# Attention and two expert layers on one core: weights and v scaled on the way to their fp16 halves

## The chip, the cores and the metric

The kernel runs on one core of a Trainium2 chip. The metric is the device time of one execution in microseconds (us), from the first to the last instruction with what the launch adds around them. Five engines work side by side: TensorE (PE, with its weight loads as PEld), VectorE (DVE), ScalarE (ACT), GpSimd (POOL) and SyncE (SP, which only issues transfers here).

## What is computed

The inputs come as float64 (the generator's weights) or float32 and the kernel keeps fp32-like precision by splitting each operand into two fp16 halves, a high and a low one, and multiplying three of the four pairs.

```python
def _attn_ref(q, k, v, proj):            # q, k, v: (2, 8, 768, 64)
    q_bits = (q @ proj > 0); k_bits = (k @ proj > 0)      # 6 bits: a bucket
    mask = q_bucket[:, :, :, None] == k_bucket[:, :, None, :]
    scores = np.where(mask, q @ k.T / sqrt(D), -1e9)
    return softmax(scores) @ v
def _moe_ref(x, w1, w2, w3, w_out):      # x: (1536, 512), d_ff 768
    h = np.maximum(np.maximum(x @ w1, x @ w2), x @ w3)
    return h @ w_out
def _moe2_ref(x, w_in, w_out):           # d_ff 2048
    h = x @ w_in
    return np.where(h > 0, h, np.exp(np.minimum(h, 0)) - 1) @ w_out
```

The output is `_moe2_ref(_moe_ref(_attn_ref(...)))`, 1536 x 512 in fp32.

## The kernel before

**Stages.** The tokens are cut into six chunks of 256. Attention runs over 24 units (a pair of heads of a chunk), four tiles each, 96 tiles of 128 queries in all. Per tile: four score matmuls on PE into the ring `s` (L646), the row maximum on DVE (L649), the scale and bias on DVE (L650, L652), the exponential on ACT into `P` (L654), the high half `hl` of `P` as a cast on ACT or DVE (L660, L662), the low half as a subtraction on POOL or DVE (L665), one transposing transfer `PT<-hl` (L667), and the products with v on PE (L676, L677). A chunk of four units is normalised, split, transposed into `xT`, and goes through the first expert layer (`plan_moe1`, matmuls at L714 with the operands `w` and `wot`). When all 96 tiles are done the attention's buffers are closed (`close_attn`) and the second layer (`plan_moe2`) runs over four groups of four 128-column slices of its weights, each group over the six chunks: matmuls L714 (`win`) and L848 (`wo2t`).

**Weights.** There are 56 weight tiles of 128x512 (18 of w1, w2, w3, 6 of `wot`, 16 of `win`, 16 of `wo2t`). They arrive as float64, 512 KB each. `plan_w` turns a tile into fp32: ACT writes a rebiased word `t1` (L558; the ring `dc1w` or `dc` in SBUF, two buffers), two half-word operations fill `t2` (L562 or L563, and L566 or L567, on ACT or DVE), and DVE joins `t1` and `t2` (L569). A norm follows (for the first 24 a Gram matrix on PE, L345; for the other 32 a square on ACT, L378) and from it a power-of-two scale. `plan_wsplit` then scales the tile in place (L580 on ACT or L581 on DVE), rounds it to the fp16 high half (L582, ACT or DVE), and subtracts to get the low half (L584, POOL or DVE). `plan_v` treats each of the eight 128x768 tiles of v alike (L524 to L527).

**Order.** Nothing here is ordered by hand. Every operation is declared with the engines it may run on, a cost on each, and a priority; a list scheduler (`Graph.schedule`) walks its own model of time, gives each engine the ready operation of the lowest priority number, and so fixes engine and order for the whole program before it runs. Each engine then runs its list in order. An operation marked `two=True` is one that the scheduler keeps from running on DVE while POOL works, unless `KAPPA` says that the delay is cheap. Rings limit what can run ahead: `mo`, three PSUM banks, is shared by the matmuls of both expert layers, the transposes of q and k, the Gram matrices and the norms.

**Line numbers.** In the changed file most lines after `plan_v` stand one line higher; L649 there is L648, L582 is L581 or L582, L584 is L583.

Of the kernel before, what the change touches and what calls it, by code (L numbers as in the profile page):

```python
# [233 lines left out]
KAPPA = 0.00184  # L234
# [4 lines left out]
def lsh_attention_moe_kernel(ctx: ExitStack, tc: tile.TileContext, q, k, v, proj,  # L239
# [80 lines left out]
    def sumsq(cols, prio, cap=False, also=(), x2=None, wt=None):  # L320
# [10 lines left out]
        op({"PE": 30 * (len(cols) + cap)}, mm, rd=[d for d, _ in cols], wr=[x2, c] + list(also), prio=prio + -6.12)  # L331
        return x2, c

    def gram(srcs, n, prio, cap=False, also=()):
# [13 lines left out]
        op({"PE": pe(len(srcs) * n // 128, 128)}, mm, rd=[b for b, _ in srcs], wr=[x2, m] + list(also), prio=prio + -10.78)  # L348
        op({"V": vred(128)}, lambda e: V.tensor_reduce(out=m.ap, in_=x2.ap[:, 0:128], op=ALU.max, axis=AX.X), rd=[x2], wr=[m], prio=prio + -0.87)
# [10 lines left out]
    def pow2(x2, s, inv, T, prio):  # L360
# [4 lines left out]
                                                       op0=ALU.logical_shift_right), rd=[x2], wr=[c], prio=prio + -9.83)  # L365
        op({"V": TINY}, lambda e: V.tensor_scalar(out=s[1]().bitcast(I32), in0=c.ap, scalar1=-u, scalar2=(189 + T) * u,
                                                  op0=ALU.mult, op1=ALU.add), rd=[c], wr=[s[0]], prio=prio + -1.03)
        op({"V": TINY}, lambda e: V.tensor_scalar(out=inv[1]().bitcast(I32), in0=c.ap, scalar1=u, scalar2=(65 - T) * u,
                                                  op0=ALU.mult, op1=ALU.add), rd=[c], wr=[inv[0]], prio=prio + 26.71)
# [4 lines left out]
    def square(src, sfn, n, acc, prio):  # L374
# [5 lines left out]
        op({"A": act(n, acc=1)}, f, rd=[src], wr=[acc[0]], prio=prio + -15.84)  # L380


    def plan_proj(prio):
        pr, acc, ps, pinv = tn(NB, "pr", 1), tn(1, "pacc", 1), tn(1, "ps", 1), tn(1, "pinv", 1)
        t0, t1 = tn(NB, "pt0", 1), tn(NB, "pt1", 1)
        op({"A": (640, 640, 30, -363.79)}, lambda e: A.dma_start(out=pr.ap[0:64], in_=proj), wr=[pr], prio=prio + -31.29)
        op({"A": (640, 640, 30, 99.65)}, lambda e: A.dma_start(out=pr.ap[64:128], in_=proj), wr=[pr], prio=prio + 49.41)
# [6 lines left out]
           rd=[pr, ps], wr=[t0], two=True, prio=prio + -24.51)  # L394
        op({"V": TINY}, lambda e: V.tensor_scalar(out=h[:, 0], in0=t0.ap, scalar1=-c, scalar2=None, op0=ALU.add),
           rd=[t0], wr=["prh0"], two=True, prio=prio + -184.42)
        op({"V": TINY}, lambda e: V.scalar_tensor_tensor(out=t1.ap, in0=pr.ap, scalar=ps.ap[:, 0:1], in1=h[:, 0],
                                                         op0=ALU.mult, op1=ALU.subtract), rd=[pr, ps, "prh0"], wr=[t1], two=True, prio=prio + -85.35)
        op({"V": TINY}, lambda e: V.tensor_copy(h[:, 1], t1.ap), rd=[t1], wr=["prh1"], two=True, prio=prio + -83.86)
        op({"V": TINY}, lambda e: V.tensor_tensor(out=h[:, 2], in0=t1.ap, in1=h[:, 1], op=ALU.subtract),  # L400
           rd=[t1, "prh1"], wr=["prh2"], two=True, prio=prio + -12.54)
# [398 lines left out]
    def plan_moe2(c, gi, fs, p0, dp):  # L800
# [54 lines left out]
        for j in range(QT):  # L855
# [8 lines left out]
            if gi == len(GROUPS) - 1:  # L864
                op({"D": (475, 450, 728)}, lambda e, j=j, ot=ot: SP.dma_start(out=dst[:, hf * QT + j, :], in_=ot.ap), rd=[ot], prio=pr + -42.11)
# [17 lines left out]
    for f in range(FM):  # L883
        plan_w13(f, CS + LM + 3 * f * DM1 - LW)
# [78 lines left out]
```

## Time and profile before

| | us |
|---|---|
| median of 3 runs (705.98 to 707.42) | 707.23 |
| the profiled execution's own time | 701.04 |
| its span, first to last instruction | 699.3 |
| PE busy | 623.1 (89%) |
| DVE busy | 580.2 (83%) |
| ACT busy | 495.0 (71%) |
| POOL busy | 287.3 (41%) |

The busy times of the table are sums over the whole span, while the stages are limited by different engines, so they are to be read per stretch: the page's slices (forty of 17.5 us each) and the windows (busy time of each engine in a stretch that one chooses) do that. The mean granted clock of TensorE is 0.941 of full speed. A row of instructions by line gives the count, the summed busy time and the mean duration of one; consecutive instructions of one engine overlap by about 0.1 us in these records, so sums of means are a little larger than the time that the engine was taken.

### The profile page before, as it was taken

Reading aid. Unit: us, or ns where it says so; the run is one execution under the profiler, and the core shown is the slowest. Engines: PE = TensorE matmul, PEld = TensorE weight load, DVE = VectorE, ACT = ScalarE, POOL = GpSimd, SP = SyncE. Lnnn points to the kernel's source line nnn. Section 1 sums busy time; section 2 is a strip of 40 time slices with the busy share of each in tenths; the row PEclk is TensorE's granted clock in tenths of the full one; section 3 lists DMA queues with packets and bytes.
Section 4 is the critical chain, followed back from the end, with each engine's and each line's share of the span. In section 5 each row is a group of like instructions: output and inputs, shape, how many; then the busy total and the mean of one; then the engine's idle time right before and its main releaser. Section 6 shows DMA issues by size and latency. Waiting matters only on the chain.

```text
span 699.3 us, 15296 instructions
## 1 busy us (share of the span) xinstructions
PE 623.1 (89%) x5658; PEld 473.4 (68%) x5658; DVE 580.2 (83%) x1594; ACT 495.0 (71%) x992; POOL 287.3 (41%) x231
## 2 busy tenths in 40 slices
PE   4586646878999969999999999999999999999997
PEld 3354434667788858888888887766666666666664
DVE  6798787978999969878999878778878978997774
ACT  4799999978998846775576369967945993763332
POOL 1366766556878743463454213512301440350000
PEclk9858677998899989999999999999999999999999
DMA  7899899995899868596798785311310210000112
GB/s 228 242 210 203 209 215 208 189 190 98 151 200 178 147 112 145 92 164 117 132 160 134 139 234 175 121 61 35 118 31 29 94 61 1 1 1 1 61 39 82
DMA packets 201210, 87.57 MB, mean 125 GB/s; under 512 B 167856, under 2 KB 195504, under 8 KB 201136
## 3 DMA queue, kind: packets, MB, share of 16 engines
q1 hardware_dynamic: 194768, 79.89, 54.0%
q10 hardware_dynamic: 6368, 6.70, 3.3%
q8 instruction: 44, 0.72, 0.4%
q14 instruction: 30, 0.25, 0.1%
HBM read 38.80 MB, written 3.15 MB: 60 GB/s over the span
## 4 chain that ended last, share of the span: by engine, by line
PE 65%; ACT 15%; DVE 8%; DMA 8%; issue 3%; POOL 0%; SPq 0%; ACTq 0%; DVEq 0%; POOLq 0%
PE mo L714 34%; PE out L848 17%; PE s L646 7%; PE o L676 3%; ACT P L654 3%; DMA PT<-hl 3%; DMA rawv<-in_v_dram 2%; ACT junk L378 2%; DMA raww<-in_moe_w_out_dram 2%; ACT hl L660 2%; PE o L677 2%; ACT dc2w L580 1%; DVE m L649 1%; PE mo L345 1%; PE mo L458 1%
## 5 line engine op out<-in xcount | busy, mean ns | idle before, releaser
L665 POOL TENSOR_TENSOR hl<-P,hl 128x768 f16<-128x768 f32 x80 | 135.5, 1699 | 100.8 <-ACT hl L660 66.6
L714 PE MATMUL mo<-xT,w 128*128 128x256 f16 x1296 | 154.0, 274 | 0.7 <-DVE hx L735 0.7
L714 PE MATMUL mo<-x1T,win 128*128 128x256 f16 x1152 | 140.6, 272 | 0.7 <-POOL win L584 0.7
L848 PE MATMUL out<-wo2t,gt 128*128 128x512 f16 x576 | 138.3, 379 | 0.0
L714 PEld LDWEIGHTS <-w 128*128 128x128 f16 x1296 | 123.8, 98 | 18.5 <-issue 2.0
L714 PEld LDWEIGHTS <-win 128*128 128x128 f16 x1152 | 111.0, 98 | 31.5 <-issue 1.3
L654 ACT ACTIVATE P<-s,bias,scale 128x768 f32<-128x768 f32 x96 | 94.4, 984 | 25.5 <-DVE bias L652 19.4
L842 POOL TENSOR_TENSOR gt<-g,gt 128x256 f16<-128x256 f32 x42 | 30.5, 728 | 176.1 <-ACT gt L840 150.5
L833 ACT ACTIVATE r<-mo,nih 128x256 f32<-128x256 f32 x96 | 45.1, 470 | 80.6 <-PE mo L714 75.0
L649 DVE TENSOR_REDUCE m<-s 128x1 f32<-128x768 f32 x96 | 90.2, 947 | 4.8 <-PE s L646 2.5
L848 PEld LDWEIGHTS <-gt 128*128 128x128 f16 x576 | 56.1, 98 | 49.6
L676 PE MATMUL o<-vt,PT 128*128 128x128 f16 x576 | 65.0, 229 | 23.9 <-DMA PT<-hl 20.3
L676 PEld LDWEIGHTS <-PT 128*128 128x128 f16 x576 | 54.3, 103 | 29.3 <-DMA PT<-hl 26.9
L646 PE MATMUL s<-ka,qa 128*128 128x384 f16 x192 | 54.3, 370 | 17.0 <-ACT P L654 16.6
L836 DVE TENSOR_SCALAR uu<-e,sg 128x256 f32<-128x256 f32 x96 | 39.7, 413 | 32.2 <-ACT e L835 31.6
L660 ACT CAST hl<-P 128x768 f16<-128x768 f32 x74 | 61.2, 830 | 5.2 <-DMA PT<-hl 3.8
L677 PE MATMUL o<-vt,PT 128*128 128x64 f16 x576 | 62.7, 201 | 0.0
L646 PE MATMUL s<-kb,qb 76*128 76x384 f16 x192 | 54.5, 369 | 2.3 <-DMA qb<-btq 1.7
L677 PEld LDWEIGHTS <-PT 128*128 128x128 f16 x576 | 53.0, 102 | 4.4 <-issue 2.5
L714 PE MATMUL mo<-hT,wot 128*128 128x256 f16 x432 | 52.1, 278 | 1.9 <-ACT hx L767 1.9
L714 PEld LDWEIGHTS <-wot 128*128 128x128 f16 x432 | 42.6, 100 | 8.5 <-issue 2.1
L838 DVE SCALAR_TENSOR_TENSOR g<-mo,aj,uu 128x256 f32<-128x256 f32 x96 | 45.8, 479 | 1.5
(197 smaller groups left out, 1147.6 us busy)
## 6 DMA issues: line engine op xcount, KB each, us to landing
raww<-in_moe_w_dram SPq DMA_DIRECT2D x16, 512.0 KB
raw<-in_moe_w_in_dram SPq DMA_DIRECT2D x15, 512.0 KB
raw<-in_moe_w_out_dram SPq DMA_DIRECT2D x14, 512.0 KB
out_dram<-ot SPq DMA_DIRECT2D x12, 256.0 KB
rawv<-in_v_dram SPq DMA_DIRECT2D x7, 384.0 KB
rawk<-in_k_dram SPq DMA_DIRECT2D x6, 384.0 KB
rawq<-in_q_dram SPq DMA_DIRECT2D x9, 256.0 KB
raww<-in_moe_w_out_dram SPq DMA_DIRECT2D x4, 512.0 KB
```

The lines of the kernel that those rows point to most:

```text
L646: PE.matmul(ps.ap[:, h, :NK], lh[0:n, h0 + i, j], rh[0:n, i, h * CH:(h + 1) * CH], start=first, stop=not first)
L649: op({"V": vred(S)}, lambda e: V.tensor_reduce(out=m.ap, in_=ps.ap[:, :, :NK], op=ALU.max, axis=AX.XY), rd=[ps], wr=[m], prio=t + 6.59)
L654: op({"A": act(S, ap=2, acc=1) - 42}, lambda e: A.activation(out=P.ap.rearrange("p (c n) -> p c n", c=2), in_=ps.ap[:, :, :NK], func=AF.Ex ...
L660: A.copy(hl.ap[:, 0], P.ap)
L665: op({"G": gtt(S), "V": (vtt(S), 86.15)}, lambda e: eng[e].tensor_tensor(out=hl.ap[:, 1], in0=P.ap, in1=hl.ap[:, 0], op=ALU.subtract), rd= ...
L676: PE.matmul(oo, pt.ap[:, kt], vt.ap[:, :, i, kt], start=(kt == 0), stop=False)
L677: PE.matmul(oo[:, 0], pt.ap[:, NS + kt], vt.ap[:, 0, i, kt], start=False, stop=(kt == NS - 1))
L714: PE.matmul(o, lh(kk, x), rh(kk, y), start=(kk == 0 and pi == 0), stop=(kk == n - 1 and pi == 2))
L833: op({"A": act(NQ, ap=1) - 42}, lambda e, m=m, o=o, r=r: A.activation(out=r.ap, in_=o.ap[:, :NQ], func=AF.Relu, scale=nih.ap[:, m:m + 1]), ...
L836: op({"V": vts(NQ)}, lambda e, m=m, ex=ex, uu=uu: V.tensor_scalar(out=uu.ap, in0=ex.ap, scalar1=-1.0, scalar2=sg.ap[:, m:m + 1], op0=ALU.a ...
L838: op({"V": vstt(NQ)}, lambda e, m=m, o=o, uu=uu, gg=gg: V.scalar_tensor_tensor(out=gg.ap, in0=o.ap[:, :NQ], scalar=aj.ap[:, m:m + 1], in1= ...
L848: PE.matmul(outs[j].ap, gt.ap[:, x, j * 128:(j + 1) * 128], wo2t[f].ap[:, y], start=(m == 0 and pi == 0), stop=(m == n - 1 and pi == 2))
```

## The change

Three things change in the code, and then the numbers that set the order.

1. `plan_wsplit`: the pass that scaled a weight tile in place is gone. The high half is scaled and rounded in one instruction (ACT or DVE), and the low half is one DVE instruction, tile times scale minus high half. POOL no longer takes part.
2. `plan_v`: the same for the tiles of v.
3. `plan_w`: `t1` goes to PSUM: to the ring `mo` for the first 24 tiles, and to a bank of its own (`t1p`, one buffer) for the 32 of the second layer. The joining instruction L569 then reads one operand from PSUM, and is no longer marked `two`.
4. Nearly all priorities, some costs, `KAPPA` and the due times of the weights are new numbers. A line of them stands below; the places that matter follow as orders.

```diff
-KAPPA = 0.00184
+KAPPA = 0.03535
@@ plan_v
-        op({"A": act(N, ap=1), "V": (vts(N), 116.51)}, ... out=raw.ap, in_=raw.ap, func=AF.Copy, scale=s) ...
-        op({"A": act(N), "V": (vcopy(N), 110.7)}, ... (V.tensor_copy if e == "V" else A.copy)(flat(0), raw.ap), ...
-        op({"G": gtt(N), "V": (vtt(N), 96.11)}, ... tensor_tensor(out=flat(1), in0=raw.ap, in1=flat(0), op=ALU.subtract), ...
+        op({"A": act(N, ap=1), "V": (vts(N), -141.22)}, ... out=flat(0), in_=raw.ap, func=AF.Copy, scale=s) ...
+        op({"V": vstt(N)}, ... scalar_tensor_tensor(out=flat(1), in0=raw.ap, scalar=s, in1=flat(0), op0=ALU.mult, op1=ALU.subtract), ...
@@ plan_w
-        raw, t1, t2 = ..., ring(pool, [128, 512], "dc1" + tag, 2, ordered=True), ...
+        raw, t1, t2 = ..., mo() if tag == "w" else ring(lambda: late["ps_t"], [128, 512], "t1p", 1), ...
-           rd=[t1, t2], wr=[t2], two=True, prio=prio + -8.05)
+           rd=[t1, t2], wr=[t2], prio=prio + -6.8)
@@ plan_wsplit
-        op({"A": act(512, ap=1), "V": (vts(512), 143.43)}, ... out=w(), in_=w(), func=AF.Copy, scale=s[1]()) ...
-        op({"A": act(512), "V": (vcopy(512), 6.61)}, ... (V.tensor_copy if e == "V" else A.copy)(dfn(0), w()), ...
-        return op({"G": gtt(512), "V": (vtt(512), 14.87)}, ... tensor_tensor(out=dfn(1), in0=w(), in1=dfn(0), op=ALU.subtract), ...
+        op({"A": act(512, ap=1), "V": (vts(512), 129.55)}, ... out=dfn(0), in_=w(), func=AF.Copy, scale=s[1]()) ...
+        return op({"V": vstt(512)}, ... scalar_tensor_tensor(out=dfn(1), in0=w(), scalar=s[1](), in1=dfn(0), op0=ALU.mult, op1=ALU.subtract), ...
@@ close_attn
+        late["ps_t"] = ctx.enter_context(tc.tile_pool(name="ps_t", bufs=1, space=PSUM, reuse_waits="tile"))
@@ the due times (one line of many)
-            plan_w2(f + m, (p0 - 15.13 if gi else M2 - 6.72) + m * 2 * 1.72, 1.72)
+            plan_w2(f + m, (p0 - W2L if gi else M2 - W2F) + m * 2 * W2S, W2S)
```

The first place is DVE ahead of the first row maximum of attention, `m<-s`. `dc2w` is `t2` of a weight tile, `vt` the halves of v, `natk` and `natq` the halves of k and q. Before:

```order
L446 TENSOR_SCALAR natq<-rawq 128x8x64
L364 TENSOR_SCALAR p2c<-mo 128x1
L349 TENSOR_REDUCE gm<-mo 128x1
L366 TENSOR_SCALAR vs_92<-p2c 128x1
L569 SCALAR_TENSOR_TENSOR dc2w<-dc1w,dc2w 128x512
L526 CAST vt<-rawv 128x768
L569 SCALAR_TENSOR_TENSOR dc2w<-dc1w,dc2w 128x512
L649 TENSOR_REDUCE m<-s 128x1
```

The same place on DVE in the changed program:

```order
L563 TENSOR_SCALAR dc2w<-raww 128x512
L582 TENSOR_SCALAR w_98<-dc2w,swm 128x512
L476 TENSOR_REDUCE zq<-mo 128x48
L583 SCALAR_TENSOR_TENSOR w_98<-dc2w,swm,w_98 128x512
L364 TENSOR_SCALAR p2c<-mo 128x1
L480 TENSOR_SCALAR bitsq<-zq 128x8x6 x2
L569 SCALAR_TENSOR_TENSOR dc2w<-mo,dc2w 128x512
L446 TENSOR_SCALAR natk<-rawk 128x12x64
L366 TENSOR_SCALAR vs_93<-p2c 128x1
L368 TENSOR_SCALAR vs_93<-p2c 128x1
L448 TENSOR_TENSOR natk<-rawk,natk 128x12x64
L648 TENSOR_REDUCE m<-s 128x1
```

Six joined weight tiles, two finished low halves of w and four low halves of v now stand on DVE ahead of the first row maximum, where there were three, none and none.

The second place is POOL in the first third of attention, between the low halves `hl` of `P`. Before:

```order
L584 TENSOR_TENSOR w_98<-dc2w,w_98 128x512
L665 TENSOR_TENSOR hl<-P,hl 128x768
L584 TENSOR_TENSOR w_98<-dc2w,w_98 128x512 x2
L665 TENSOR_TENSOR hl<-P,hl 128x768 x2
L584 TENSOR_TENSOR w_98<-dc2w,w_98 128x512 x3
L665 TENSOR_TENSOR hl<-P,hl 128x768
L448 TENSOR_TENSOR natk<-rawk,natk 128x12x64
L665 TENSOR_TENSOR hl<-P,hl 128x768
```

The same place on POOL in the changed program:

```order
L664 TENSOR_TENSOR hl<-P,hl 128x768 x4
L696 TENSOR_TENSOR xf<-xs,r 128x256
L699 TENSOR_TENSOR xn<-xf,xn 128x256
L664 TENSOR_TENSOR hl<-P,hl 128x768 x2
L448 TENSOR_TENSOR natk<-rawk,natk 128x12x64
L664 TENSOR_TENSOR hl<-P,hl 128x768 x2
L696 TENSOR_TENSOR xf<-xs,r 128x256
```

The low halves of the weights are gone from POOL, and two short steps of the attention's output (`xf`, `xn`) that mostly ran on DVE stand between the `hl` instead.

## Rows read from the trace of the kernel before

**Rows 1.** The page's slices of 17.5 us, busy tenths, and the granted clock

```profile
PE   4586646878999969999999999999999999999997
ACT  4799999978998846775576369967945993763332
...
PEclk9858677998899989999999999999999999999999
```

**Rows 2.** Windows: stretch, length; busy us PE, PEld, DVE, ACT, POOL; PEclk, DMA share, GB/s

```profile
0.00:27.00 27.00, 12.87 (x112) 9.61 (x113) 19.16 (x78) 15.65 (x26) 7.21 (x11) 1.00 0.73 216
27.00:193.50 166.50, 120.24 (x1169) 90.34 (x1168) 140.94 (x360) 150.20 (x269) 106.02 (x72) 0.77 0.91 192
50.00:150.00 100.00, 68.33 (x674) 50.62 (x674) 84.72 (x200) 92.52 (x165) 66.67 (x46) 0.77 1.00 210
193.50:400.00 206.50, 198.01 (x2258) 168.38 (x2255) 181.71 (x432) 137.73 (x258) 107.30 (x78) 0.98 0.82 141
400.00:475.00 75.00, 71.56 (x603) 57.60 (x603) 59.07 (x187) 57.45 (x128) 21.18 (x20) 1.00 0.47 145
425.00:450.00 25.00, 23.01 (x201) 18.87 (x200) 18.97 (x63) 24.97 (x57) 12.45 (x12) 1.00 0.48 149
475.00:650.00 175.00, 175.00 (x1229) 118.42 (x1228) 147.96 (x458) 118.58 (x277) 44.28 (x50) 1.00 0.12 37
```

**Rows 3.** Windows, row maxima of line L649 alone: stretch, length, busy us (count)

```profile
0.00:193.50 193.50, 37.80 (x40) 0.81 0.88 195
```

**Rows 4.** The chain of waits from 50 us: start us, us, what

```profile
70.20 0.67 ACT dc2w L562
...
73.48 1.05 ACT P L654 x2
74.53 1.46 ACT hl L660 x2
76.02 1.01 POOL hl L665
77.05 3.85 DMA PT<-hl
```

**Rows 5.** Groups by line and shape, ACT: count | busy us, mean ns | idle before

```profile
L580 ACT ACTIVATE dc2w<-dc2w,swm 128x512 f32<-128x512 f32 x18 | 12.1, 711 | 1.5 <-DVE p2c L364 1.5
L582 ACT CAST w<-dc2w 128x512 f16<-128x512 f32 x13 | 7.6, 603 | 0.0
L566 ACT ACTIVATE dc2w<-raww 128x512 f16<-128x512 f32 x16 | 12.4, 774 | 1.0 <-DVE natk L446 1.0
L524 ACT ACTIVATE rawv<-rawv,vs 128x768 f32<-128x768 f32 x7 | 6.5, 929 | 0.0
```

**Rows 6.** Single lines on DVE: ns min/median/max, first and last start us

```profile
L569 DVE SCALAR_TENSOR_TENSOR dc2w<-dc1w,dc2w x24: 672/693/2143, 15.5 to 156.5; 128x512 int32<-128x512 int32 x24
L735 DVE SCALAR_TENSOR_TENSOR hx<-mo,hx x36: 675/683/693, 136.3 to 433.6; 128x512 f32<-128x512 f32 x36
L563 DVE TENSOR_SCALAR dc2w<-raww x11: 440/454/1710, 14.0 to 144.3; 128x512 uint16<-128x512 uint16 x11
```

**Rows 7.** Groups by line and shape, DVE and POOL, columns as in rows 5

```profile
L569 DVE SCALAR_TENSOR_TENSOR dc2w<-dc1w,dc2w 128x512 int32<-128x512 int32 x24 | 25.2, 1056 | 9.1 <-ACT dc2w L566 6.5 <-POOL w L584 2.5
L563 DVE TENSOR_SCALAR dc2w<-raww 128x512 uint16<-128x512 uint16 x11 | 8.2, 754 | 0.4 <-DMA raww<-in_moe_w_out_dram 0.4
L582 DVE CAST w<-dc2w 128x512 f16<-128x512 f32 x5 | 3.3, 708 | 0.0
L584 DVE TENSOR_TENSOR w<-dc2w,w 128x512 f16<-128x512 f32 x3 | 2.6, 882 | 0.7 <-ACT w L582 0.7
L448 DVE TENSOR_TENSOR natk<-rawk,natk 128x768 f16<-128x768 f32 x6 | 7.0, 1174 | 0.0
L697 DVE TENSOR_TENSOR xf<-xs,r 128x256 f32<-128x256 f32 x19 | 11.3, 592 | 0.1
L584 POOL TENSOR_TENSOR w<-dc2w,w 128x512 f16<-128x512 f32 x15 | 19.7, 1325 | 4.4 <-ACT w L582 2.3 <-DVE w L582 2.0
```

More of the change, by code (lines that the diff above doesn't have):

```diff
@@ L329, in mm @@
                 PE.matmul(x2.ap[:, 0:1], ones, capc, start=False, stop=True)
-        op({"PE": 30 * (len(cols) + cap)}, mm, rd=[d for d, _ in cols], wr=[x2, c] + list(also), prio=prio + -6.12)
+        op({"PE": 30 * (len(cols) + cap)}, mm, rd=[d for d, _ in cols], wr=[x2, c] + list(also), prio=prio + -8.9)
         return x2, c
@@ L346, in mm @@
                     k += 1
-        op({"PE": pe(len(srcs) * n // 128, 128)}, mm, rd=[b for b, _ in srcs], wr=[x2, m] + list(also), prio=prio + -10.78)
-        op({"V": vred(128)}, lambda e: V.tensor_reduce(out=m.ap, in_=x2.ap[:, 0:128], op=ALU.max, axis=AX.X), rd=[x2], wr=[m], prio=prio + -0.87)
+        op({"PE": pe(len(srcs) * n // 128, 128)}, mm, rd=[b for b, _ in srcs], wr=[x2, m] + list(also), prio=prio + -0.85)
+        op({"V": vred(128)}, lambda e: V.tensor_reduce(out=m.ap, in_=x2.ap[:, 0:128], op=ALU.max, axis=AX.X), rd=[x2], wr=[m], prio=prio + -55.77)
         return sumsq([bufcol(m)], prio, cap, also, x2, ones3)
@@ L406, in plan_proj @@
                     op({"V": TINY}, lambda e, t=t, w=w, rows=rows, part=part: V.tensor_copy(pbt[rows, t, w], h[rows, part]),
-                       rd=[f"prh{part}"], wr=["pb"], two=True, prio=prio + 41.48)
+                       rd=[f"prh{part}"], wr=["pb"], two=True, prio=prio + 65.66)
     K, Q, qinv, kinv, first = {}, {}, {}, {}, {}
@@ L756, in plan_moe1 @@
         pow2(x2, bufcol(ch, 0), bufcol(ch, 1), -2, pr)
-        op({"V": TINY}, lambda e: V.tensor_tensor(out=sx[c], in0=sh[b], in1=ch.ap, op=ALU.mult), rd=[f"sh{b}", ch], wr=[f"sx{c}"], two=True, prio=pr + 102.16)
+        op({"V": TINY}, lambda e: V.tensor_tensor(out=sx[c], in0=sh[b], in1=ch.ap, op=ALU.mult), rd=[f"sh{b}", ch], wr=[f"sx{c}"], two=True, prio=pr + 316.79)
         xx = x1T[c]
@@ L836, in plan_moe2 @@
+            op({"A": act(NQ)}, lambda e, r=r, ex=ex: A.activation(out=ex.ap, in_=r.ap, func=AF.Exp, scale=-1.0), rd=[r], wr=[ex], prio=pr + -434.34)
             op({"V": vts(NQ)}, lambda e, m=m, ex=ex, uu=uu: V.tensor_scalar(out=uu.ap, in0=ex.ap, scalar1=-1.0, scalar2=sg.ap[:, m:m + 1],
-                                                                            op0=ALU.add, op1=ALU.mult), rd=[ex, sg], wr=[uu], two=True, prio=pr + -154.51)
+                                                                            op0=ALU.add, op1=ALU.mult), rd=[ex, sg], wr=[uu], two=True, prio=pr + -365.42)
@@ L845, in omm @@
+            op({"V": vcopy(NQ), "A": (act(NQ), -274.45)}, lambda e, gg=gg, gt=gt: (V.tensor_copy if e == "V" else A.copy)(gt.ap[:, 0], gg.ap),
+               rd=[gg], wr=[gt], two=True, prio=pr + -502.96)
+            op({"G": gtt(NQ), "V": (vtt(NQ), -318.75)}, lambda e, gg=gg, gt=gt: eng[e].tensor_tensor(
+                out=gt.ap[:, 1], in0=gg.ap, in1=gt.ap[:, 0], op=ALU.subtract), rd=[gg, gt], wr=[gt], two=True, prio=pr + -520.58)
             def omm(e, f=f, m=m, gt=gt):
@@ L881, in lsh_attention_moe_kernel @@
             plan_vmin(b, t0 - LV)
-    DM1 = 0.3959
+    DM1 = 0.191
+    DW1 = 0.0092
+    CM = 0.0249
+    W2S = -8.5598
+    W2L = -11.9988
+    W2F = 1891.5629
     for f in range(FM):
-        plan_w13(f, CS + LM + 3 * f * DM1 - LW)
-    plan_wo(CS + LM + 18 * DM1 - LW)
+        plan_w13(f, CS + LM + 3 * f * DW1 - LW)
+    plan_wo(CS + LM + 18 * DW1 - LW)
     for t in range(NT):
```

228 lines of the change are left out of this document (110 added, 118 removed).

## The prediction, made before the changed kernel ran

> **What bounds the kernel now.** I read the slices first [rows 1]. From about 200 us on, the PE line stands at 9 nearly everywhere; before that it reads 4 to 8, and there the ACT line reads 9. So the program has two parts: a late one in which TensorE works without a gap, where nothing that other engines save can be cashed, and an early one in which it waits. The windows put numbers to it [rows 2]. From 475 to 650 us PE is busy 175.0 of 175 us. From 193.5 to 400 it is 198.0 of 206.5, from 400 to 475 it is 71.6 of 75. But from 27 to 193.5 us it is 120.2 of 166.5, at a mean granted clock of 0.77, so part of it at the lower of the two levels (1.2 GHz), after the idle stretches. Some 46 us of idle TensorE lie in that early stretch, and 8.5 and 3.4 in the next two. I cut at 193.5 because the 40th of 96 row maxima ends there [rows 3], and because both programs have issued the same first-layer matmuls by the 40th score (216 with `w`, 72 with `wot`), though the new order has 132 instead of 192 of the former by the 32nd score. Whatever time the 40th score is moved by, the end is moved by, unless the late part loses it.
>
> What limits the early stretch? In it ACT is busy 150.2 of 166.5 us (90%), DVE 140.9 (85%), the DMA engines 91%, and between 50 and 150 us even 100% [rows 2]. The chain of waits there runs from one ACT instruction to the next (a weight's `dc2w`, an exponential, a cast) and changes to a transfer `PT<-hl` now and then [rows 4]. So ACT ends last most often, DMA is behind it, DVE is third, and each would hold the others not far below the present time.
>
> **The change, part by part.** I counted in both orders what ACT and DVE issue up to the 40th score; durations are the means of rows.
>
> *ACT, early.* Twenty-three scaling passes go (0.711 each, 16.4) and eighteen casts of weights (0.603, 10.9); twenty scale-and-round instructions come, for which the scaling pass is the nearest row (0.711, 14.2). Ten half-word operations move to DVE (0.774, 7.7). Of v, six scalings go and two come (0.929, 3.7), with two casts (some 1.7). Three scalings of q go (some 2.2); hi-casts, small casts and evacuations that come from DVE add some 6.6. The sum is 21.8 less [rows 5]. `t1` is written 24 times as before, only to PSUM; no row shows ACT writing there, so I leave its 0.66 us alone, between 0 and the whole difference of a wait (below).
>
> *DVE, early.* Twenty-four low halves of weights come. No row shows this form; the nearest is L569, two four-byte SBUF operands of the same size, 0.693 median and 1.056 mean, the difference being a few that took up to 2.1 us [rows 6, 7]: 16.6 to 25.3. Five low halves go that DVE had (0.882, 4.4). Four low halves of v come (0.98 to 1.17 by L448's mean, 4.7). Ten half-word operations come (0.454 median to 0.754 mean, 4.5 to 7.5), four scale-and-rounds (0.42 to 0.71, 1.7 to 2.8), and six casts go (4.2). The joining L569 reads PSUM now: L735, the same operation with one operand from PSUM, takes 0.675 to 0.693 in all 36 cases, without the long ones [rows 6], so 24 times 1.056 minus 0.685, 8.9 saved, or nothing. Seven `xf` (0.592), seven `xn` and nine small copies go to POOL and ACT, three low halves of q come: some 10 less. Low end: 16.6 + 4.7 + 4.5 + 1.7 - 4.4 - 4.2 - 8.9 - 10 = 0. High end: 25.3 + 4.7 + 7.5 + 2.8 - 4.4 - 4.2 - 0 - 10 = 21.7. I take +4, near the low end, because POOL, beside whose work the long cases stand, loses 19 low halves of weights (1.325 each) and five of v by then, over 25 us of its 113 for the weights alone, and gets back a few [rows 2, 7].
>
> The Trainium skill has a sentence against this step: VectorE's microarchitecture page ("Vector Engine (DVE) Microarchitecture Reference", section 7, Points that are easy to get wrong) says that this instruction with two SBUF sources that are not bf16 runs at half rate. The trace does not bear it out: L569 with two such sources has its fastest case at 0.672 us, L735 with one of them in PSUM at 0.675 [rows 6]. By the rule the 24 low halves would add another 16.6 us (an estimate from that page's half rate and L569's median), and the 40th score would come 12.6 us late, not 5.9 early.
>
> *The 40th score.* DVE's work after 27 us becomes 144.9. If DVE then is as full as ACT was (90.2%), the stretch takes 160.6 us and the score ends at 187.6 instead of 193.5: 5.9 us earlier. ACT's remaining 128.4 would allow 169; the DMA engines' work, 0.91 of 166.5 or 151.5 us, would at 100% allow 178.5 [rows 2]. So the gain is what DVE leaves: 5.9. At DVE's low end it is 10, at its high end the score ends at 207, 13.8 later.
>
> *The first score* comes later in the new order, since twelve more large instructions for weights and v stand ahead of it on DVE. I cost that at nothing beyond the sum: the same work is then missing behind it. If that cover is gone, because DVE is idle later for want of scores, the loss is what it puts ahead, up to 15 us, and is in the slower rival.
>
> *193.5 to 400 us.* TensorE idles 8.5 us there. The new priorities could remove that or double it; no row says which, so I take 0, with both ends.
>
> *400 to 475 us.* The second layer's first eight weight tiles are prepared while TensorE finishes the first layer. It idles 3.4 us [rows 2]; ACT is full in the middle of it (24.97 of 25). Eight casts leave ACT (0.603, 4.8), and the low halves go from POOL to DVE, which has 59 of 75. Against it, `t1p` has one buffer: ACT's next L558 now waits until DVE has joined the last one, with the matmul evacuations queued behind it on ACT. Eight such waits of 0.685 are 5.5. I take -1, between -3.4 and +5.5.
>
> *475 to 650 us.* Here some 24 low halves come to DVE (0.693, 16.6), the other additions and removals being about even: 148 becomes some 165 of 175 us (94%). TensorE has no gap to give, so no gain is possible. For the loss, ACT at 24.97 of 25 us cost TensorE 2.0 us [rows 2]; three groups of weights so make at most 6. I take +1.
>
> *Sum.* -5.9 - 1 + 1 = -5.9. The profiled execution took 701.04 us, which makes 695.1; against the median of 707.23 it is 701.3. I assume that the 6 us between that execution and the median stay.
>
> **The rivals.**
>
> *DVE becomes the bound* (slower). Place: DVE from 27 us to the 40th score. Everything on POOL's side of the exchange is now behind one in-order engine that also makes each row maximum, scale and bias, so the exponentials on ACT wait. It decides from the point at which DVE's work there reaches 150.2 us, 9.3 more than now. Halfway from there to the high end (+15.5) the stretch takes 173.4, the score ends 6.9 us late: 714. At the high end 721. For it: DVE is already at 85%, the rows that show the 2.1 us cases, and the later first score. Against it: POOL's retreat and the constant L735.
>
> *The low halves take twice their row* (slower still). Place: the 24 early low halves on DVE; each 0.693 more makes 16.6, DVE 161.5 after 27 us, the score 12.6 late: 720. L569's fastest case, 0.672, speaks against it [rows 6]. This is what the sentence quoted above from the Trainium skill's "Vector Engine (DVE) Microarchitecture Reference" would make of the time.
>
> *ACT alone was the limit* (faster). If DVE's long instructions were only waits for POOL and go with it, DVE falls below ACT and the transfers decide: the score at 178.5 to 183, 10 to 15 earlier, 692 to 697, middle 694. For it: the chain is ACT's. Against it: DVE has no room at 85%.
>
> *The ring gives it back* (no change). ACT's write of `t1` must now find one of three `mo` banks free, which it shares with everything that PE puts out. Each of 24 waits of 0.25 us would take the 5.9 back: 707. Against it: in that stretch PE is idle for 46 us, so the ring has slack most of the time.
>
> **How the numbers follow.** Forecast (697 to 706, around 701.3) 0.44; ACT alone (692 to 697) 0.19; ring, or no relief for another reason (706 to 708) 0.14; DVE the bound (708 to 721, around 714) 0.20; low halves at twice their row (720) 0.03. About 0.2%, 1.4 us, is what a measurement of this kernel can tell from no change. Faster by more: 0.41 of the forecast's 0.44, 0.19, and 0.06 of the ring's 0.14, 0.66. Slower: 0.22. Same: 0.12. Range: left out are the part of the fast rival below 692 (0.05) and of the slow ones above 715 (0.12), so 692 to 715.
>
> **What the profile will show.** Right: the 40th row maximum ends at about 188 us; between 27 us and there ACT's share falls below DVE's, DVE's is about 90%, and the joining line reads near 0.69 us without cases of 2 us; the low half of a weight takes about 0.7. PE from 475 to 650 us stays above 98%. Wrong: a low half near 1.4 us (twice its row); ACT idle ahead of the exponential, released by DVE's bias, for over 20 us early (DVE the bound); ACT idle ahead of L558, released by `mo` (the ring); TensorE below 171 of the 175 us (the late part pays). If the 40th score comes early and the time does not, the late part of the sum is wrong; if the score comes late, the DVE term is.

## The result, and the profile after

The changed kernel takes 687.61 us in the median (four runs, 686.06 to 689.24); the kernel before took 707.33 beside it (705.98 to 708.04). The ratio is 0.972, 95% interval 0.969 to 0.976: faster by 19.7 us, where the forecast was 5.9 and the range ended at 692. The profiled execution is the slowest of the four, 689.24 us with a span of 687.4, so the two traces, before and after, are only 11.9 us apart.

The page's slices of the kernel after (17.2 us each, a fortieth of the shorter span; busy tenths, granted clock), to be held against [rows 1]:

```profile
PE   3367577899999999999999999899999999999997
...
DVE  6899779899899968998998498899779889976775
ACT  4698699879877886776585168769458756533332
...
PEclk9999856999999999999999999999999999999999
```

TensorE reaches its 9s two slices earlier and keeps them but for one 8, ACT's unbroken run of 9s from the third slice on is gone, and the clock has one deep dip (5 and 6, some 86 to 120 us).

The windows of after, columns as in [rows 2], cut where its 40th row maximum ends:

```profile
27.00:184.60 157.60, 120.85 (x1200) 91.58 (x1200) 143.31 (x363) 134.64 (x245) 85.64 (x64) 0.88 0.94 196
184.60:275.00 90.40, 85.60 (x1001) 72.60 (x998) 78.61 (x189) 70.01 (x133) 54.37 (x42) 1.00 0.86 152
275.00:400.00 125.00, 123.49 (x1379) 106.10 (x1378) 103.54 (x253) 77.21 (x146) 58.28 (x45) 1.00 0.81 145
400.00:475.00 75.00, 70.91 (x559) 54.01 (x557) 68.90 (x237) 57.09 (x126) 7.61 (x9) 0.98 0.35 113
475.00:650.00 175.00, 175.00 (x1223) 118.33 (x1222) 146.44 (x465) 98.09 (x222) 20.90 (x29) 1.00 0.12 40
```

and the window of the kernel before that answers to the second of them, which [rows 2] did not cut out:

```profile
193.50:275.00 81.50, 74.70 (x858) 62.50 (x855) 72.96 (x176) 60.90 (x113) 52.22 (x37) 0.96 0.86 154
```

Busy time alone does not compare two stretches at different clocks. So I also counted matmul work in each stretch: of every PE group its count times its columns, over 2.4 GHz. Both traces hold 558.1 us of it. At the cut (193.5 before, 184.6 after) 87.8 and 88.7 us of it are done, so the cuts are the same place in the program within a microsecond. What is not work is lost, as idle time or because the clock was lower:

| stretch | lost before | lost after | change | forecast |
|---|---|---|---|---|
| to the 40th row maximum | 105.7 | 95.9 | -9.8 | -5.9 |
| from there to 400 us | 20.3 | 16.9 | -3.4 | 0 |
| 400 to 475 us | 6.6 | 8.5 | +1.9 | -1 |
| 475 us to the end | 8.6 | 8.0 | -0.6 | +1 |
| sum | 141.2 | 129.3 | -11.9 | -5.9 |

The lines that the prediction names, as single lines of DVE (ns min/median/max, first and last start us): the row maxima up to the cut, before and after, then the joining line from PSUM and the low half.

```profile
L649 DVE TENSOR_REDUCE m<-s x40: 926/948/958, 27.2 to 192.2; 128x1 f32<-128x768 f32 x40
```

```profile
L648 DVE TENSOR_REDUCE m<-s x40: 915/944/959, 40.6 to 183.6; 128x1 f32<-128x768 f32 x40
```

```profile
L569 DVE SCALAR_TENSOR_TENSOR dc2w<-mo,dc2w x24: 669/680/737, 15.8 to 145.5; 128x512 int32<-128x512 int32 x24
L583 DVE SCALAR_TENSOR_TENSOR w<-dc2w,swm,w x18: 719/740/1750, 34.4 to 142.0; 128x512 f16<-128x512 f32 x18
```

ACT's write of `t1`, late and early, and its scale-and-round, grouped by line and shape (columns as in [rows 5]):

```profile
L558 ACT ACTIVATE t1p<-raw 128x512 f32<-128x512 f32 x32 | 20.1, 629 | 0.3 <-DVE dc L569 0.3
L558 ACT ACTIVATE mo<-raww 128x512 f32<-128x512 f32 x24 | 15.0, 631 | 3.2 <-DMA raww<-in_moe_w_out_dram 2.1 <-DMA raww<-in_moe_w_dram 1.0
L581 ACT ACTIVATE w<-dc2w,swm 128x512 f16<-128x512 f32 x15 | 10.3, 712 | 0.2
```

The DVE term of the sum came out in its numbers: 143.3 us of work to the cut (forecast 144.9), 90.9% full (forecast 90.2), DVE now above ACT (134.6 of 157.6, 85%). Whether the filling is more than a coincidence is asked below. The joining line has lost its 2 us cases [rows 6]. The row maxima start 13 us later than before (40.6 against 27.2), within the 15 us that the prediction named, and still end 9 us earlier.

### The profile page after: what moved, and what is told of

Same layout as the page of the kernel before. It is cut to its first block, busy times and chain, and to the rows that moved or that the text cites. A ratio compares the mean times of both kernels' runs of the same rounds, so it can differ in the third digit from the quotient of the medians.

```text
span 687.4 us, 15209 instructions
## 1 busy us (share of the span) xinstructions
PE 619.2 (90%) x5658; PEld 472.3 (69%) x5658; DVE 581.7 (85%) x1637; ACT 463.1 (67%) x920; POOL 229.5 (33%) x196
## 4 chain that ended last, share of the span: by engine, by line
PE 59%; DMA 13%; DVE 9%; ACT 8%; POOL 4%; issue 3%; SPq 0%; ACTq 0%; DVEq 0%; POOLq 0%
PE mo L713 33%; PE out L847 18%; DMA PT<-hl 11%; PE s L645 4%; POOL hl L664 2%; PE o L675 2%; ACT P L653 2%; ACT hl L659 2%; DVE m L648 1%; DVE hx L734 1%; ACT junk L378 1%; PE o L676 1%; DMA rawk<-in_k_dram 1%; DMA raww<-in_moe_w_dram 1%; DVE hl L664 0%
## 5 line engine op out<-in xcount | busy, mean ns | idle before, releaser
L664 POOL TENSOR_TENSOR hl<-P,hl 128x768 f16<-128x768 f32 x83 | 137.2, 1660 | 92.9 <-ACT hl L659 78.4
L713 PE MATMUL mo<-xT,w 128*128 128x256 f16 x1296 | 151.7, 272 | 3.8 <-DVE hx L734 1.4
L847 PE MATMUL out<-wo2t,gt 128*128 128x512 f16 x576 | 140.0, 381 | 0.0
L713 PEld LDWEIGHTS <-w 128*128 128x128 f16 x1296 | 123.4, 98 | 19.6 <-issue 4.3
L841 POOL TENSOR_TENSOR gt<-g,gt 128x256 f16<-128x256 f32 x39 | 28.2, 724 | 237.1 <-ACT gt L839 155.1
L659 ACT CAST hl<-P 128x768 f16<-128x768 f32 x84 | 69.2, 832 | 20.9 <-DMA PT<-hl 19.6
L675 PE MATMUL o<-vt,PT 128*128 128x128 f16 x576 | 66.5, 230 | 17.8 <-DMA PT<-hl 14.2
L835 DVE TENSOR_SCALAR uu<-e,sg 128x256 f32<-128x256 f32 x96 | 34.5, 360 | 30.1 <-ACT e L834 29.6
L713 PE MATMUL mo<-hT,wot 128*128 128x256 f16 x432 | 49.4, 272 | 0.0
```

What stands on the lines that cost most here:

```text
L659: A.copy(hl.ap[:, 0], P.ap)
L664: op({"G": gtt(S), "V": (vtt(S), 203.46)}, lambda e: eng[e].tensor_tensor(out=hl.ap[:, 1], in0=P.ap, in1=hl.ap[:, 0], op=ALU.subtract), rd ...
L675: PE.matmul(oo, pt.ap[:, kt], vt.ap[:, :, i, kt], start=(kt == 0), stop=False)
L713: PE.matmul(o, lh(kk, x), rh(kk, y), start=(kk == 0 and pi == 0), stop=(kk == n - 1 and pi == 2))
L835: op({"V": vts(NQ)}, lambda e, m=m, ex=ex, uu=uu: V.tensor_scalar(out=uu.ap, in0=ex.ap, scalar1=-1.0, scalar2=sg.ap[:, m:m + 1], op0=ALU.a ...
L847: PE.matmul(outs[j].ap, gt.ap[:, x, j * 128:(j + 1) * 128], wo2t[f].ap[:, y], start=(m == 0 and pi == 0), stop=(m == n - 1 and pi == 2))
```

## The experiments

**Code and numbers apart.** First the changed code was given the old numbers (priorities, surcharges, costs, due times), and the old code the new ones; the scheduler made a new order in both.

```diff
# newcode_oldnum: code of after; every number as in before, for example
-  ..., rd=[ps, sc, bi], wr=[P, rs], prio=t + -164.62)
+  ..., rd=[ps, sc, bi], wr=[P, rs], prio=t + -2.92)
# oldcode_newnum: code of before; the reverse
```

> The changed code (scale and round in one pass, low halves on DVE, rebiased word in PSUM) with the priorities and engine surcharges of the kernel before. Theory 'less work' (the code edits took the work off the engine that bounds the first 193 us, the numbers only fit the order to it): 687 to 692 us, nearly all of the 19.7 us. Theory 'the order' (the new numbers bring the gain, the edits are a means): 702 to 710 us. Theory 'both, only together': over 697 us here and in the mirror run.

> The code of the kernel before with the new numbers where an operation has one (operations that only the code of before has keep their old number). 'Less work': 703 to 715 us, no gain. 'The order': 688 to 693 us. 'Both, only together': over 697 us.

Measured: 714.52 us (ratio to before 1.014, 1.007 to 1.020) and 732.55 (1.041, 1.034 to 1.048). Both are slower than before. Neither "less work" nor "the order" holds; the two gain only together. With the old numbers the changed code loses its time early: by the same count of matmul work 119.3 us are lost to the 40th row maximum (105.7 before) and 34.1 behind it (35.5 before).

**Which numbers?** The changed kernel with one group of old numbers at a time (early weights; attention tiles; q, k and v), and the changed code with old numbers except for one group (the two numbers of the early weight loads; all numbers of the early weights).

```diff
# after_oldw / oldnum_neww: in plan_w, plan_wsplit for the first 24 tiles, and the due times
-    DW1 = 0.0092
+    DW1 = 0.3959
# after_oldattn: all of plan_tile; after_oldqkv: plan_qk, plan_v, plan_vmin
# oldnum_newload: the load alone
-  "A": (520, 460, 1456, 241.61) ... prio=prio + 155.87
+  "A": (520, 460, 1456, 115.54) ... prio=prio + 389.26
```

> The changed kernel with the old numbers of the early weights alone (their load, unpacking, scaling and low half, and the spacing of the 24 tiles in the order). Theory 'weights earlier' (the new numbers bring 8 joins before 50 us where the changed code with the old numbers has 3, all 24 by 150 us instead of 175, so the first MoE's matmuls can fill TensorE sooner): TensorE's column work by 200 us falls from 104 us to 90 to 97, time 694 to 702 us. If the order of the attention tiles brings the gain: 686 to 690 us.

> The changed kernel with the old numbers of the attention tiles alone (score to xT: the exponentials P and the transposing DMAs lose some of their precedence). 'Weights earlier': 686 to 691 us. Theory 'attention first' (P and PT ahead of everything on their engines keeps the chain of a tile short): 697 to 707 us, with fewer than 44 row maxima by 200 us.

> The changed kernel with the old numbers of the q, k and v preparation alone. 'Weights earlier' and 'attention first' both: 686 to 692 us. If the preparation of q, k, v paces the early stretch: over 695 us.

> The changed code with the old numbers except two: the precedence and the ACT surcharge of the early weight loads are the new ones. In the changed code with all numbers old, ACT and DVE waited 24.7 us for weight loads before 200 us. If these two numbers are what the loads lacked: 698 to 706 us, with under 8 us of such waits. If the numbers only work as one set: 711 to 725 us.

> The changed code with the old numbers except those of the early weights (load, unpacking, scaling, low half, spacing), which are the new ones: the mirror of the run that put only these back. If the early weights' numbers are the part that brings the gain: 692 to 704 us. If the numbers work only as one set: 711 us or more.

Measured: 734.40, 764.67 and 710.52 us with one group put back; 714.41 and 716.72 with one group brought in. Every group that is put back costs 23 to 77 us, more than the whole gain. The two theories had named at most 702 and 707 us for the first two runs. Of the groups brought in alone only the early weights' and their loads' were tried, and they bring nothing; the attention's and those of q, k and v were not tried. The scheduler compares the priorities of all groups with each other, so a mixed set makes a third order rather than a part of one. The 40th row maximum is then no fixed place either: with the early weights' old numbers it starts at 179.5 us, 4 us earlier than in the changed kernel, with 81.1 us of matmul work done instead of 88.7, and the end comes 47 us later. The loads are a warning of their own. In the changed code with old numbers the waits of ACT and DVE before 200 us are led by weight loads (line waited for: us in total, times, longest):

```profile
ACT mo L557 <- DMA raww<-in_moe_w_dram: 12.2, 6, 3.8
ACT P L651 <- DVE bias L649: 11.1, 6, 3.2
```

```profile
DVE dc2w L562 <- DMA raww<-in_moe_w_dram: 12.5, 4, 3.8
```

The two load numbers left those waits where they were. With all of the early weights' numbers they fell to

```profile
ACT P L651 <- DVE bias L649: 12.1, 12, 3.9
ACT mo L557 <- DVE bias L649: 2.7, 1, 2.7
ACT mo L557 <- DMA raww<-in_moe_w_dram: 2.7, 3, 1.6
```

and the time did not move (716.72 against 714.52). The early stretch did: the 40th row maximum starts at 193.4 us instead of 207.4, though with 3 us less of matmul work done by then. But 48.4 us are lost behind it instead of 34.1. So removing the largest wait moved the place, and the later part gave it back. My theory "weights earlier" falls with it.

**Code exchanged, order kept.** A new order differs in many places at once, so the next kernels keep the order of one kernel and exchange only what an operation issues. In the order of before: the changed code for weights and v; its early or its late weights alone; and the early scaling passes left out. The rebiased word stays in SBUF in all four.

```diff
# before_newcode, before_newbody (first 24 tiles), before_newlate (last 32): plan_wsplit of before
-  A.activation(out=w(), in_=w(), func=AF.Copy, scale=s)      # own pass
-  A.copy(dfn(0), w())
-  G.tensor_tensor(out=dfn(1), in0=w(), in1=dfn(0), op=ALU.subtract)
+  A.activation(out=dfn(0), in_=w(), func=AF.Copy, scale=s)
+  V.scalar_tensor_tensor(out=dfn(1), in0=w(), scalar=s, in1=dfn(0), op0=ALU.mult, op1=ALU.subtract)
# before_newcode: both groups of tiles, and the same in plan_v
# before_noscale: the first line alone is dropped, for the first 24 tiles
```

> The kernel before, its order kept, with the scaling passes of the 24 early weight tiles left out (so the halves are those of unscaled weights): about 17 us less ACT work before 194 us, nothing else. Prediction's step (ACT bounds until DVE does, 5.9 us later work): 698 to 701 us. ACT's share as the put-back pass showed in the changed kernel (half of it): 695 to 698 us. ACT covered: 704 to 708 us.

> The kernel before, its order kept, with the changed early weight code in it: scale and round in one pass, low halves by DVE at the places where POOL had them (the rebiased word stays in SBUF). About 17 us off ACT, 24 x 0.82 = 20 us onto DVE, 24 x 1.3 us off POOL. If the edits alone carry a gain and the new numbers only refine it: 697 to 702 us. If DVE pays what the doubled low halves showed (0.8 of what is added) and ACT gives back half: 711 to 715 us, slower, as the changed code with the old numbers was.

> The kernel before, its order kept, with the changed code for the 32 late weight tiles alone (scale and round in one pass, low half by DVE at POOL's place). In the new order the same edit is worth 8 us. The prediction's terms for the late part (-1 and +1): 704 to 708 us, as before. If the edit saves as much in any order: 697 to 700 us.

> The kernel before, its order kept, with all the changed code for weights and v in it (the rebiased word stays in SBUF): the fourth corner beside old code in the old order (706), old code in the new order (711) and both new (688). If code and order are worth something only together: 701 to 707 us. If the edits carry the gain in any order that was made for other work: under 697 us.

Measured: 704.08 (0.997, 0.992 to 1.001), 703.39 (1.000, 0.997 to 1.003), 706.84 (1.003, 0.999 to 1.008), 701.95 us (0.995, 0.993 to 0.998). In the old order these edits are worth 3.6 us at most. Leaving out the scaling passes alone gains 1.4 us against 705.5, and its interval includes no gain at all: this is the range for "ACT covered", not that for the prediction's step. The row maxima, without the scaling passes and then with the changed early weights:

```profile
L649 DVE TENSOR_REDUCE m<-s x40: 925/947/959, 27.2 to 186.8; 128x1 f32<-128x768 f32 x40
```

```profile
L665 DVE TENSOR_REDUCE m<-s x40: 926/946/959, 26.3 to 193.3; 128x1 f32<-128x768 f32 x40
```

Against the trace of before (27.2 to 192.2) the 40th row maximum starts 5.4 us earlier and 1.1 us later. But both traces are the fastest of their ten executions, the first by far (695.87 us, with a median of 704.08), and two executions of one and the same early program lie nearly as far apart: with the late weights alone exchanged nothing is changed before 415 us, and there the 40th row maximum starts 3.6 us later than in the trace of before.

```profile
L665 DVE TENSOR_REDUCE m<-s x40: 926/945/958, 26.9 to 195.8; 128x1 f32<-128x768 f32 x40
```

So neither difference shows more than that these edits, in this order, bring little.

In the order of after: all of the old code; its early weights, late weights or v alone; and the scaling passes alone. The late rebiased word stays in PSUM in all of them.

```diff
# after_oldcode, after_oldbody (first 24 tiles, dc1w in SBUF), after_oldlate (last 32), after_oldv
+  A.activation(out=w(), in_=w(), func=AF.Copy, scale=s)
+  A.copy(dfn(0), w())
+  G.tensor_tensor(out=dfn(1), in0=w(), in1=dfn(0), op=ALU.subtract)
# three_pass: the first two lines alone, first 24 tiles; the low half stays on DVE
```

> The changed kernel, its order kept, with the early weight code of before in it: scaling pass of its own on ACT, low halves on POOL, rebiased word in SBUF; only the order (and v, and the later weights) stays new. If the order carries the gain whatever the code: 688 to 697 us. If the code carries it: 703 to 712 us. By the slopes seen (ACT +17.1 at 0.5, DVE -20 at 0.8, word in SBUF +2): 682 to 688 us, so a version faster than both, if POOL keeps up with 24 x 1.3 us more.

> The changed kernel, order kept, with the scaling pass back and the low halves on POOL for the 32 late weight tiles (after 380 us). TensorE is over 98% full from 475 us, so: 687 to 690 us if only the transition from 400 to 450 us can feel it, 691 to 696 us if the transition is paced by these tiles (2.5 us were lost there).

> The changed kernel, order kept, with the v code of before: each of the 8 v tiles scaled in a pass of its own (8 x 0.9 = 7 us of ACT) and its low half on POOL (8 x 1.8 us) instead of DVE (8 x 1.07 us). Theory 'the order made the stretch from the 40th to the 96th row maximum 10.5 us shorter, whatever the code': 688 to 692 us, that stretch within 2 us of 184.7. Rival 'v's edit made it shorter': 693 to 698 us, that stretch 190 us or more.

> The changed kernel, order kept, with all the code of before in it: early and late weights and v in three passes with low halves on POOL, the early rebiased word in SBUF (the late one stays in PSUM). What is left against the kernel before is the order alone. From the early part alone (700.4 us): 700 to 704 us if v and the late weights cost nothing, up to 712 us if they cost what the early ones do for each tile (0.5 us).

> The changed kernel, order kept, with the scaling of the 24 early weight tiles put back as an ACT pass of its own (24 more of 0.711 us = 17.1 us of ACT work before 194 us). If ACT bounds the early stretch: 40th row maximum 15 to 19 us later, time 700 to 706 us. If DVE or the transposing DMAs bound it: 688 to 692 us.

Measured: 700.40, 695.62, 688.65, 711.07 and 696.19 us. Against 687.61 the early weights' edit, with their word in PSUM, is worth 12.8 us in this order (8.6 of it the scaling pass), the late weights' 8.0, v's 1.0 (not clear of the noise), all together 23.5. My slopes, which promised 682 to 688 us for the early weights' code of before, do not add up: 700.40. And v is not what shortened the stretch from the 40th to the 96th row maximum: 185.8 us with its old code, 184.8 in the changed kernel, 195.1 before. Of these 10.3 us, some 6 are matmul work that the new order leaves for later.

The four corners, medians:

| | old code | new code |
|---|---|---|
| order of before | 705.5 (80 runs) | 702.0 |
| order of after | 711.1 | 687.6 |

They are not quite square. The new code in the order of before has all its rebiased words in SBUF, and the old code in the order of after has the late ones in PSUM. With the early word in SBUF the order of after takes 689.7 us (below), so the way from 705.5 leads by the edits in the old order to 702.0 (-3.6), by the new order, with the late words in PSUM, to 689.7 (-12.3), and by the early word in PSUM to 687.6 (-2.1, about as large as its own uncertainty).

Where the corners differ, by the count of matmul work (us lost to the 40th row maximum, and behind it; one trace each):

| | old code | new code |
|---|---|---|
| order of before | 105.7 and 35.5 | 106.3 and 37.3 |
| order of after | 108.5 and 43.1 | 95.9 and 33.4 |

A second execution of the upper left corner's early program (the run with late weights alone) loses 109.2. So early, three corners are alike, and only the new code in the new order is some 10 us better. Behind the 40th row maximum it is the old code in the new order that stands apart, 6 to 10 us worse.

The early edit shows in the 40th row maximum, 183.6 with the new code (above) and here with the scaling passes back:

```profile
L659 DVE TENSOR_REDUCE m<-s x40: 923/947/959, 41.0 to 192.6; 128x1 f32<-128x768 f32 x40
```

The late edit shows in TensorE's waits from 400 us on, first before, then in the kernel after, then with the late weights in three passes:

```profile
PE mo L327 <- ACT junk L378: 0.6, 2, 0.5
```

```profile
PE mo L327 <- ACT junk L378: 2.0, 3, 0.8
PE mo L713 <- DVE p2c L364: 1.1, 1, 1.1
```

```profile
PE mo L327 <- ACT junk L378: 5.6, 6, 1.8
PE mo L727 <- DVE g L851: 1.6, 4, 0.9
```

TensorE stands at the small norm matmuls and waits for ACT's squares (5.6 us instead of 2.0, of the 7.7 us between the two traces). That the squares come late because they queue behind the extra passes is the likely reason, not a shown one; the single buffer of `t1p` is not it (0.4 us of waiting ahead of its 32 writes). From 475 to 650 us TensorE is busy 171.7 of 175:

```profile
475.00:650.00 175.00, 171.74 (x1195) 115.69 (x1193) 144.47 (x449) 105.10 (x234) 39.93 (x46) 1.00 0.11 37
```

The kernel before, with the same three passes (and the late word in SBUF), had 175.0 there [rows 2]. Its order left room for the passes; the new one does not.

**Which engine bounds the early stretch now?** Two more in the order of after: the early rebiased word back in SBUF, and each early low half issued twice.

```diff
# t1_sbuf
+  if tag == "w":
+      t1.make = lambda: wpre.tile([128, 512], F32, tag="dc1w", bufs=2)
# low_twice, first 24 tiles: the line stands twice
   V.scalar_tensor_tensor(out=dfn(1), in0=w(), scalar=s, in1=dfn(0), ...)
+  V.scalar_tensor_tensor(out=dfn(1), in0=w(), scalar=s, in1=dfn(0), ...)
```

> The changed kernel, order kept, with the early rebiased word back in an SBUF ring of two; the joining operation should take 1.06 us again instead of 0.68 (24 x 0.372 = 8.9 us more DVE work before 194 us, PSUM's mo ring relieved of 24 tiles). If DVE bounds the early stretch: 695 to 698 us. If ACT or the transfers bound it: 686 to 690 us. If the mo ring was what held it: below 686 us.

> The changed kernel, order kept, with each of the 24 early low halves issued twice on DVE: 24 x 0.82 = 19.7 us more DVE work before 150 us, result unchanged. DVE is the bound at 90% full, as the prediction had it: 40th row maximum 20 us later, 706 to 710 us. DVE shares the stretch with ACT as the ACT pass put back showed (8.6 us for 17.1): 696 to 699 us. DVE is covered: 687 to 691 us.

Measured: 689.67 and 709.93 us. The DVE lines behind it, word in SBUF first, then the doubled low halves:

```profile
L571 DVE SCALAR_TENSOR_TENSOR dc2w<-dc1w,dc2w 128x512 int32<-128x512 int32 x24 | 20.9, 870 | 0.7 <-ACT dc2w L568 0.6
```

```profile
L583 DVE SCALAR_TENSOR_TENSOR w<-dc2w,swm,w 128x512 f16<-128x512 f32 x36 | 32.2, 900 | 0.6
L583 DVE SCALAR_TENSOR_TENSOR wot<-dc2w,wosc,wot 128x512 f16<-128x512 f32 x12 | 13.7, 1149 | 0.2
```

The joining line did not go back to the 1.06 us that I expected but to 0.870. Its word in SBUF adds 4.5 us by these groups (20.9 less 16.4) and costs 2.1.

How much an added us costs is better read from the page's busy times, since sums of groups count the overlap of consecutive instructions and long cases that come and go. In order: the kernel after, the scaling passes put back, the doubled low halves.

```profile
PE 619.2 (90%) x5658; PEld 472.3 (69%) x5658; DVE 581.7 (85%) x1637; ACT 463.1 (67%) x920; POOL 229.5 (33%) x196
```

```profile
PE 616.2 (89%) x5658; PEld 470.4 (68%) x5658; DVE 581.7 (84%) x1641; ACT 474.0 (68%) x940; POOL 230.6 (33%) x196
```

```profile
PE 624.7 (88%) x5658; PEld 476.0 (67%) x5658; DVE 602.3 (85%) x1661; ACT 463.0 (65%) x920; POOL 232.9 (33%) x196
```

The scaling passes add 10.9 us to ACT and nothing to DVE (the rounding beside them is shorter, 0.618 against 0.712 us), and cost 8.6. The doubling adds 20.6 us to DVE and costs 22.3; of that, 18.7 us are there at the 40th row maximum:

```profile
L648 DVE TENSOR_REDUCE m<-s x40: 919/945/959, 41.4 to 202.3; 128x1 f32<-128x768 f32 x40
```

So in the new order an added us costs 0.8 on ACT and about 1.1 on DVE. The "half" for ACT in the expectations above came from counting 17.1 us as added. Neither engine alone sets the pace: each delays the end nearly in full while the other's work stays as it is.

The word in SBUF also gives the fairest comparison of the two orders, since the early code is then the same. From 27 us to the end of the 40th row maximum, in the order of before and in that of after (columns as in [rows 2]):

```profile
27.00:193.80 166.80, 117.48 (x1158) 88.86 (x1155) 148.71 (x377) 136.56 (x241) 77.09 (x51) 0.77 0.87 190
```

```profile
27.00:184.80 157.80, 120.68 (x1172) 90.71 (x1172) 148.13 (x357) 133.82 (x244) 88.54 (x63) 0.86 0.91 195
```

DVE's work is the same and ACT's nearly so, but the stretch is 9.0 us shorter: DVE is 93.9% full instead of 89.2%.

## Why the prediction was wrong

Two steps failed: the assumption on the base, and the terms that set the new order to nothing. All the signs that the prediction listed as right came true (the early 40th row maximum, DVE near 90%, the joining line without 2 us cases, a low half of 0.7 us, TensorE full from 475 us), and the time was still outside the range: they test the pieces of the sum, not these two steps.

**The base.** "I assume that the 6 us between that execution and the median stay" failed. Counted by the two traces it is the largest single error: 7.8 of the missing 13.7 us. The kernel before was run 80 more times beside the experiments and lay between 697.7 and 711.8 us (median 705.5). Its profiled execution (701.0) was one of the faster draws, 4.5 us under that median; that of after (689.2) was the slowest of four, 1.6 above theirs; and the 707.2 of the forecast lay 1.7 above the 705.5. The fastest third of the 80 had a mean granted clock of 0.937, the slowest third 0.929, so the spread goes along with the granted clock; which brings about which is not shown. The two traces of one early program (before, and before with late weights exchanged) place it: of the 5.1 us between their spans, 3.5 are lost ahead of the 40th row maximum. So the traces, 11.9 us apart, understate the gain between typical executions, which is 17.9 us (705.5 to 687.6). A gain read between two executions of such a kernel is uncertain by several us whatever the traces say.

**The order at nothing.** The prediction priced the edits (-5.9) and gave the new numbers no term of their own: the first score's delay at "nothing beyond the sum", 193.5 to 400 us at "no row says which, so I take 0". By the runs the edits are worth 3.6 us in the old order and the early word in PSUM 2.1, together close to the 5.9; the new order under the same early code is worth 12.3. That is the term that was missing. It is counted by medians, so it takes in what the traces show as the base's 6.1 us (4.5 and 1.6) and is not to be added to it.

**The 40th score.** Forecast 5.9 us earlier, measured 8.9. ACT was relieved and DVE became the fuller engine, as forecast, and work and filling of DVE were both hit within 2%, which still is 3 us in a stretch of 157.6. But that the filling came out at ACT's old 90.2% is luck. The runs show that it is no constant: 84.6% before, 89.2% with the edits in the old order, 90.9% after, 93.9% after with the word in SBUF. Nor does DVE's work alone set the stretch: with the scaling passes put back DVE's work to the 40th row maximum stays at 143.4 us and the stretch is 9.0 us longer. ACT, at 145.7 us there, still counts. The run without the scaling passes in the old order does not support the step either: its times gain 1.4 us, and its trace's 5.4 is not clear of the draw. The parts of the DVE term were less close than their sum: the joining line did drop to 0.68, as at the low end, but the 24 low halves took 19.6 us (14.8 and 4.8), not 16.6. The half-rate sentence of the Trainium skill ("Vector Engine (DVE) Microarchitecture Reference", section 7) is not borne out by these rows either: L583 with two SBUF sources, one fp32 and one fp16, has a median of 0.740 us beside 0.680 for L569 with one operand in PSUM. The first score came 13 us later and the 40th still 9 us earlier, so no loss from that shows.

**193.5 to 400 us** was set to 0, since no row says what new priorities do. They brought 3.4, all of it before 275 us (13.8 us lost before, 10.2 after). There TensorE idles less (4.8 of 90.4 us against 6.8 of 81.5), and the rest goes with the clock, granted at 0.96 before and 1.00 after. The end 8.5 of the range covered it.

**400 to 475 us** was forecast 1 us better and came 1.9 worse. `t1p`'s single buffer, the reason I gave for a loss, is not it: ACT waited 0.3 us in all ahead of its 32 writes to `t1p`. TensorE idled 4.1 us against 3.4, and 2.0 us of that against 0.6 at norm matmuls for ACT (the lists above); the rest of the 1.9 goes with the clock (0.98 against 1.00).

**475 to 650 us**: DVE came to 146.4, not 165 (84%, not 94%), and TensorE to 175.0. No loss, as the sum said within 1 us, but "nothing that other engines save can be cashed" holds only for an order that has room. In the new one the late edit is worth 8.0 us.

**The rivals.** "ACT alone was the limit" gave the nearest time (692 to 697), but its reason is refuted: DVE did not fall below ACT. "DVE becomes the bound" (714) gives the time of the changed code with the old numbers, 714.5 us, and DVE's work there, 152.8 us, is above the 150.2 that the rival named. But the 40th row maximum ends at 208, not 200, at a filling of 84%, and ACT waits 11.1 us for the bias, not over 20: the number agrees, the mechanism is not shown. The new numbers avoided that time. "The low halves take twice their row" and "the ring gives it back" are both refuted (0.740; ACT's idle time ahead of its 24 writes to `mo` is 3.2 us, and for loads).

**What stays open.** Why the edits are worth 3.6 us in one order and 23.5 in the other is followed to its places but not to its cause. Early, the new order fills DVE further with the same work (93.9% against 89.2%); late, it leaves no room for the old code's passes. Which operations stand differently so that this comes about no run shows. Of the three groups of numbers none can be put back alone, two were never brought in alone, and when the wait that looked like the cause was removed, the later part took the time back.

## What to carry to other kernels

Where a table sets the order, an edit has no price of its own: nearly the same edits were worth 3.6 and 23.5 us, and the new table cost 5.6 us with the old code and gained 14.4 with the new (12.3 without the early word in PSUM). Sum the bound engine's work for the code, as here, but do not carry one engine's filling over to another, and give the retuned order a term with a range at least as wide as the idle time in the stretch, not a zero. Before adding a difference to a median, ask how far single executions of that kernel lie apart, and do the same before reading a few us from one trace. And test a wait by removing it before calling it the cause.

## What the hardware showed unexpectedly

ACT writes 128x512 fp32 faster to PSUM than to SBUF: 0.631 us a tile against 0.663 for the same line before, and against 0.663 again in the order of after with only the word moved back to SBUF.

DVE's joining line has cases up to 2.1 us with both operands in SBUF and none above 0.74 with one in PSUM, with either table of numbers. The long cases stand beside POOL's work: in the order of after with the word in SBUF, six of the 24 take more than 0.75 us, and every one of the six overlaps an instruction of POOL. At the same place in the kernel after, also beside POOL, the PSUM form is not longer than elsewhere (start us, us; first SBUF, then PSUM):

```profile
119.18 1.55 DVE L571 SCALAR_TENSOR_TENSOR dc2w<-dc1w,dc2w 128x512 int32<-128x512 int32 x1
```

```profile
119.46 0.69 DVE L569 SCALAR_TENSOR_TENSOR dc2w<-mo,dc2w 128x512 int32<-128x512 int32 x1
```

The mean granted clock was 0.97 after and 0.94 before. Less idle time of TensorE is not the whole reason: with the scaling passes put back it idles 65.0 us to the 40th row maximum, against 60.4 before and 54.1 after, and the clock is 0.97 all the same. Nor does the new order by itself narrow the spread of executions: ten of one kernel lie within 3.1 us (doubled low halves) and 5.4 us (old early weights) in the order of after, and within 3.7 (new code), 5.9, 7.4 and 13.5 us (without the scaling passes) in that of before.
